# A linear-attention and MLP kernel: other dummy matmuls at the start, input loads in larger pieces, one bias load moved behind the transposes

## The chip, the cores and the metric

The kernel runs on one core of one Trainium2 chip. The metric is the device time of one execution in microseconds (us). The profile gives, for one profiled execution, the span from the first to the last instruction of the core, and the start and length of every instruction and DMA packet.

Engines are named as in the profile: PE (TensorE matmuls), PEld (its weight loads), DVE (VectorE), ACT (ScalarE), POOL (GpSimd), SP (SyncE, which here only issues DMAs). "SPq" and "ACTq" are the instruction queues of SP and ACT when they issue a DMA.

## The reference

One sequence of 2048 rows and 512 columns in bf16 passes through four residual steps, A, B, A, B, with the same weights in both rounds:

```python
x = x + A(layernorm(x))     # linear attention, 32 heads of 16
x = x + B(layernorm(x))     # layernorm again, 512 -> 1792, gelu, 1792 -> 512
x = x + A(layernorm(x))
x = x + B(layernorm(x))

# A: q, k, v = y @ wqkv; phi(t) = (t > 0 ? t + 1 : exp(t)) + 1e-6
#    kv = phi(k)^T v, z = sum of phi(k) over the rows
#    o = phi(q) kv / (phi(q) z + 1e-6); A = o @ wo
# B: gelu(layernorm(y) @ w1 + b1) @ w2 + b2
```

The sums over all rows in kv and z mean that phi(k) of every row has to be there before any row of A's output can be made.

## The kernel before

The 2048 rows are 16 tiles of 128 rows, four tiles to a chunk of 512. Everything stays in on-chip memory between the steps. The work is recorded as a graph of operations, and the order of the operations on each of the five engines is written out as five lists of names in `CONF["ORDER"]` (from line 325). The program plays each list in that order and inserts a semaphore wait wherever an operation reads or overwrites what another engine or a DMA made. A scheduling pass with estimated durations only gives out buffers and PSUM banks; it changes no order. So an operation that waits holds up everything behind it in its engine's list, SP's list of DMAs included.

Only the first stage, the attention half of the first round, matters for what follows. Names end in the tile number (12 to 15 first, since chunk 3 is taken first, then 0 to 11):

- **The loads.** SP issues, in this order: `x0` (tile 12, 128 KB, line 642), `x1` (tile 13, 128 KB, line 644), `wk0` (half of the key columns of wqkv, 256 KB, line 648), `x2` (tiles 14 and 15, 256 KB), `wq` (all query columns, 512 KB, line 651), and the three other chunks of x, `xc0` to `xc2` (512 KB each, line 638). ACT issues the second half of the key columns, `wk1`, after DVE has written `onesm`.
- **The dummies.** `warm` (lines 678 to 682) is the first entry of PE's list: seven matmuls of 128x512 and one of 128x128 on the tile `onesm`, whose result nobody reads. `onesm` is filled with 1.0 by DVE (`ones`, line 641), so `warm` waits for DVE.
- **Norm and turn.** For each tile the statistics are made on DVE (or ACT), the tile is centred or normalised, and it is then transposed ("turned"): tiles 12, 13, 14, 15 and 1 by PE (`PTA0_n`, line 783, copied out by ACT in `tcA0_n`, line 793), the eleven others by a DMA transpose that SP issues (`TA0_n`, line 770).
- **Keys and queries.** `K0_n` (line 838, four matmuls of 128x512) makes the keys of a tile. `Q0_c_k` (lines 856 and 869) makes queries. ACT makes exp and relu of the result (lines 808 and 819), DVE or POOL joins them to phi (`mink`, `phik`, lines 812 to 825).
- **Sums.** `G0_n` (line 939) multiplies the normalised tile with phi(k) and accumulates in four PSUM banks; `Z0_c` (line 920) sums phi(k). `zb0` (line 1000) prepares the denominators, for which `D0_...` (line 1063) are the first matmuls.
- **SP's list in this stage**, after the loads: `TA0_0 TA0_3 TA0_2 TA0_8 TA0_4 b2 TA0_6 TA0_7 TA0_5 TA0_10 TA0_11 TA0_9 b1 Tb1`. Here `b2` (line 1193) loads the bias b2 into all partitions (128 KB); it is first read by `b20_1`, which starts at 64.5 us.
- **Late loads.** wv, wo, w1 and w2 are issued by POOL (line 665) once all turns of the stage have landed.

After this stage PE's list holds the output of the attention (line 1087), the two MLP matmuls (lines 1119 and 1157) and the second round, in one mixed order.

Of the kernel before, what the change touches and what calls it, by code (L numbers as in the profile page):

```python
# [264 lines left out]
def assign_waits(graph, order, sems, dma_sems):  # L265
# [56 lines left out]
    C0=(3, 0, 1, 2), N_WARM=7, ZC=(0, 3), LQ='sp', N_HALF=1, N_K=4, N_Q=3, P_Z0=6.15, N_PB=1, N_PT=8, P_DEN=-50.43,  # L322
    P_A2=-55.11, P_W1=38.59, P_W2=10.23, P_K=55.79, P_G=131.85, P_Q=170.13, STEP=3.86, A1_Q=12.91, A1_STEP=0.5, N_H=4,
    N_N=3, GAP=28.61,
    ORDER={
        "pe":
            "warm PTA0_12 PTA0_13 K0_12 K0_13 PTA0_14 Q0_3_0 Q0_3_2 PTA0_15 K0_14 G0_12_0 Q0_3_1 K0_15 G0_13_0 "
            "G0_14_0 Q0_3_3 PTA0_1 K0_0 K0_1 G0_15_0 K0_3 G0_0_0 K0_2 Q0_0_2 Q0_0_0 G0_1_0 K0_8 Z0_3 K0_4 G0_2_0 "
            "K0_6 G0_3_0 Q0_0_3 K0_7 K0_5 G0_4_0 K0_10 K0_11 Z0_0 K0_9 Q0_1_2 Q0_1_3 Z0_1 Q0_0_1 Q0_1_0 Z0_2 "
            "G0_5_0 G0_6_0 D0_0_3 D0_0_0 G0_7_0 Q0_1_1 D0_0_1 G0_8_0 D0_0_2 G0_9_0 G0_10_0 G0_11_0 G0_11_2 G0_11_1 "  # L330
            "D0_1_0 Q0_2_0 G0_11_3 KV0_0 KV0_1 D0_1_1 ZR0 KV0_2 KV0_3 Q0_2_1 D0_1_2 M0_0 M0_1 M0_2 M0_3 Q0_2_2 "
            "WO0_0_0 WO0_0_1 WO0_0_2 WO0_0_3 D0_1_3 WO0_1_0 WO0_2_0 WO0_3_0 Q0_2_3 WO0_4_0 WO0_7_0 WO0_6_0 PTB0_0 "
            "WO0_5_0 W10_0_5_0 W10_0_1_0 W10_0_9_0 W10_0_6_0 W10_0_2_0 W10_0_3_0 W10_0_12_0 W10_0_7_0 W10_0_0_0 "
            "W10_0_4_0 W10_0_13_0 W10_0_11_0 W10_0_8_0 W10_0_10_0 W20_0_0 W20_1_0 W20_0_7 W20_1_7 W10_0_9_1 "
            "W10_0_1_1 W10_0_7_1 W10_0_8_1 W10_0_5_1 W10_0_6_1 W10_0_12_1 W10_0_0_1 W10_0_13_1 W10_0_3_1 "
            "W10_0_11_1 W10_1_4_0 W10_1_13_0 W10_0_4_1 W10_1_11_0 W10_1_0_0 W10_1_3_0 W10_1_2_0 W10_0_2_1 "
            "W10_1_6_0 WO0_9_0 WO0_8_0 WO0_11_0 W10_1_5_0 W10_1_8_0 W10_1_10_0 WO0_10_0 W10_0_10_1 W10_1_1_0 "
            "W10_1_12_0 W10_1_7_0 W10_1_9_0 W20_7_0 W20_4_0 W20_7_7 W20_4_7 WO0_15_0 W20_5_0 W20_2_0 W20_5_7 "
            "W20_6_0 W10_2_5_0 W10_2_0_0 K1_1 W20_6_7 W20_2_7 K1_0 W10_2_11_0 W10_2_10_0 WO0_12_0 WO0_14_0 "
            "WO0_13_0 W10_2_3_0 W10_2_13_0 W10_2_4_0 W10_2_2_0 W10_2_1_0 W10_2_6_0 W10_2_12_0 W10_2_9_0 W10_2_8_0 "  # L340
            "W10_2_7_0 W20_8_0 W20_9_0 W20_8_7 W20_9_7 W20_3_0 W20_10_0 K1_4 W20_3_7 K1_2 W20_10_7 W10_3_5_0 "
            "W20_11_0 W10_3_7_0 W10_3_1_0 W10_3_8_0 W10_3_3_0 W10_3_10_0 W10_3_0_0 W20_11_7 W10_3_9_0 K1_3 "
            "W10_3_6_0 W10_3_13_0 W10_3_2_0 K1_8 W10_3_11_0 W10_3_12_0 W10_3_4_0 K1_5 G1_0_1 G1_0_3 K1_6 G1_0_0 "
# [6 lines left out]
            "W11_0_1_0 W11_0_7_0 W11_0_9_0 WO1_7_0 W11_0_8_1 W11_0_4_1 W11_0_10_1 W11_0_8_0 W11_0_1_1 W11_0_5_1 "  # L350
# [23 lines left out]
            "gelu0_1_1_0 gelu0_1_9_0 gelu0_0_10_1 gelu0_1_7_0 gelu0_1_12_0 normB0_11 normA1_1 normB0_9 expk1_1 "  # L374
            "expk1_0 gelu0_2_10_0 reluk1_0 gelu0_2_5_0 gelu0_2_0_0 gelu0_2_3_0 gelu0_2_11_0 gelu0_2_13_0 "
            "gelu0_2_2_0 gelu0_2_4_0 gelu0_2_1_0 gelu0_2_6_0 gelu0_2_8_0 gelu0_2_12_0 normB0_13 gelu0_2_7_0 "
            "gelu0_2_9_0 normA1_2 expk1_2 reluk1_2 reluk1_4 gelu0_3_7_0 gelu0_3_1_0 gelu0_3_8_0 normA1_5 normA1_6 "
            "gelu0_3_0_0 gelu0_3_3_0 gelu0_3_5_0 gelu0_3_9_0 gelu0_3_10_0 reluk1_3 normA1_7 gelu0_3_6_0 "
            "gelu0_3_2_0 expk1_3 expk1_8 expk1_4 gelu0_3_13_0 gelu0_3_11_0 gelu0_3_4_0 gelu0_3_12_0 expk1_5 "
            "reluk1_8 expk1_6 reluk1_6 normA1_9 normA1_10 expk1_7 reluk1_7 normA1_11 expk1_9 expk1_10 reluk1_10 "  # L380
# [4 lines left out]
            "expq1_2_1 expq1_2_0 expq1_3_3 reluq1_2_0 reluq1_2_1 normB1_1 tcB1_1 reluq1_3_3 tcB1_0 gelu1_0_13_0 "  # L385
# [12 lines left out]
            "statsA0_15 mink0_12 yscA0_13 aggrA0_15 phik0_12 cenA0_15 mink0_13 vepsA0_14 statsA0_0 minq0_3_0 "  # L398
# [3 lines left out]
            "statsA0_7 normA0_4 aggrA0_7 phiq0_3_1 aggrA0_10 mink0_3 statsA0_5 mink0_2 aggrA0_5 phik0_2 phik0_3 "  # L402
            "statsA0_9 aggrA0_9 zs0_3 statsA0_11 aggrA0_11 mink0_8 minq0_3_3 mink0_4 phik0_8 phiq0_3_3 phik0_4 "
            "normA0_9 minq0_0_2 normA0_11 phiq0_0_2 mink0_6 mink0_7 phik0_7 minq0_0_3 phiq0_0_3 mink0_5 zs0_0 "
            "phik0_5 mink0_10 phik0_10 minq0_0_0 mink0_11 phik0_11 zs0_1 mink0_9 minq0_1_2 phik0_9 phiq0_0_0 "
# [3 lines left out]
            "RA0_4 normB0_0 minq0_2_2 minq0_2_1 RA0_7 b20_1 phiq0_2_1 RA0_5 statsB0_7 minq0_2_3 statsB0_5 "  # L409
# [21 lines left out]
            "normB1_0 rec1_1_3 statsB1_3 pr1_1_3 minq1_3_3 RA1_5 aggrB1_3 normB1_2 RA1_4 normB1_3 RA1_6 pz1_3_1 "  # L431
            "phiq1_3_2 red1_3_1 statsB1_5 statsB1_4 RA1_7 aggrB1_4 statsB1_6 den1_3_1 rec1_3_1 aggrB1_5 statsB1_7 "
            "minq1_2_0 minq1_2_1 aggrB1_7 phiq1_3_3 aggrB1_6 phiq1_2_0 red1_3_0 den1_3_0 red1_3_2 pr1_3_1 den1_3_2 "
            "pz1_2_0 normB1_5 rec1_3_0 red1_2_0 phiq1_2_1 red1_3_3 rec1_3_2 pz1_2_1 minq1_2_3 RB1_3 den1_3_3 "
            "pr1_3_0 RB1_0 den1_2_0 minq1_2_2 pr1_3_2 phiq1_2_3 pz1_2_3 rec1_2_0 red1_2_1 pr1_2_0 b21_1 phiq1_2_2 "
            "red1_2_3 RA1_13 den1_2_3 b21_5 den1_2_1 rec1_3_3 pr1_3_3 rec1_2_3 rec1_2_1 RB1_1 pz1_2_2 red1_2_2 "
            "RA1_14 den1_2_2 statsB1_13 rec1_2_2 pr1_2_2 RA1_12 statsB1_12 aggrB1_12 RB1_2 RA1_11 statsB1_14 "
            "RA1_15 statsB1_15 aggrB1_14 RA1_10 normB1_14 RA1_8 aggrB1_15 statsB1_10 statsB1_11 aggrB1_13 RA1_9 "
            "aggrB1_10 statsB1_8 normB1_13 statsB1_9 aggrB1_11 aggrB1_9 b21_7 b21_13 RB1_7 aggrB1_8 b21_12 RB1_4 "
            "normB1_8 normB1_10 RB1_5 b21_6 b21_8 b21_9 RB1_6 RB1_12 RB1_14 RB1_10 RB1_9 RB1_8 b21_11 RB1_13 "  # L440
            "RB1_11 RB1_15_0 RB1_15_1",
        "pool":
            "bdm0 id0 id1 neghalf powA0_12 vepsA0_13 powA0_13 powA0_14 eps6 vepsA0_0 powA0_15 b1z powA0_0 vepsA0_1 "
            "vepsA0_3 powA0_3 nmrA0_3 powA0_1 vepsA0_6 vepsA0_2 powA0_2 vepsA0_8 powA0_6 powA0_8 nmrA0_8 nmrA0_6 "
            "vepsA0_4 powA0_4 vepsA0_7 vepsA0_10 powA0_7 nmrA0_7 powA0_10 vepsA0_5 powA0_5 nmrA0_10 nmrA0_5 "
            "vepsA0_11 vepsA0_9 powA0_11 powA0_9 phik0_6 wo w2_1 bdm1 wv w1_1 w2_0 w1_0 phiq0_1_2 phiq0_1_1 "
            "pr0_0_2 pr0_1_0 pr0_1_1 pr0_1_2 pr0_1_3 vepsB0_1 powB0_1 vepsB0_0 powB0_0 pz0_2_1 vepsB0_2 phiq0_2_3 "
            "powB0_2 vepsB0_7 vepsB0_3 powB0_7 powB0_3 vepsB0_5 vepsB0_6 powB0_5 powB0_6 vepsB0_4 powB0_4 pr0_2_1 "
            "phiq0_2_2 b20_0 b20_3 b20_2 b20_5 vepsB0_9 vepsB0_8 vepsA1_0 powB0_8 powB0_9 vepsA1_1 powA1_0 pr0_3_3 "
            "vepsB0_10 powA1_1 pz0_3_2 vepsB0_11 nmrB0_9 powB0_11 nmrB0_11 powB0_10 nmrA1_1 b20_9 pr0_3_1 vepsA1_7 "  # L450
            "vepsA1_4 vepsB0_14 vepsB0_15 vepsB0_13 powB0_14 powB0_13 vepsB0_12 vepsA1_2 vepsA1_5 powA1_7 nmrB0_13 "
            "powB0_15 powA1_4 powB0_12 powA1_2 b20_8 b20_12 nmrA1_2 powA1_5 vepsA1_9 powA1_9 nmrA1_5 vepsA1_8 "
            "vepsA1_6 powA1_8 powA1_6 nmrA1_7 nmrA1_9 nmrA1_6 vepsA1_3 powA1_3 za1_1 vepsA1_10 za1_3 vepsA1_11 "
            "powA1_10 nmrA1_10 phik1_6 powA1_11 za1_5 phik1_7 nmrA1_11 vepsA1_13 powA1_13 za1_7 vepsA1_12 za1_8 "
            "powA1_12 nmrA1_12 za1_9 za1_10 vepsA1_14 vepsA1_15 powA1_14 powA1_15 za1_11 phik1_15 pz1_1_0 pr1_0_0 "
# [72 lines left out]
def build_kernel(nc, A_x, A_wqkv, A_wo, B_x, B_w1, B_b1, B_w2, B_b2, out, conf=None, report=False):  # L528
# [5 lines left out]
    with ExitStack() as es:  # L534
# [143 lines left out]
        def warm(e):  # L678
            for n in [D] * cf["N_WARM"] + [P]:
                ins = e.matmul(bank(wu, n), lhsT=onesm[:, 0:P], rhs=onesm[:, 0:n], start=True, stop=True)  # L680
# [671 lines left out]
```

## Time and profile before

| what | us |
|---|---|
| median of three runs | 329.73 |
| lowest and highest of them | 328.83, 329.91 |
| the profiled execution: its own time | 330.35 |
| its span | 328.6 |
| first matmul of `warm` starts | 1.51 |
| first turn on PE (`PTA0_12`) starts | 4.59 |
| `wk0` lands, `K0_12` starts | 6.43, 6.52 |
| `x0`, `x1`, `x2`, `wq` land | 3.21, 3.93, 6.95, 8.45 |
| last turn of the stage lands (`TA0_9`) | 36.95 |
| last matmul starts its stream, last DVE operation ends | about 325.8, 326.5 |

Around the span the profiled execution has 1.75 us more, which is start and end of the program.

How to read the views. The chain of work is followed back from the last instruction: at each step to what released it. A row of it is start, length, engine and line. A row of the timeline is start, length, engine, line, operation, the tiles written and read, shape and count, and in brackets the idle time of the engine before it with what ended that. The table by stretches gives for each engine the busy time and in brackets the number of instructions that started. A matmul's length in the timeline includes a modelled drain, so rows of PE overlap; how fast PE really goes is read from the distance between the starts.

### The profile page before, as it was taken

To read this page: it belongs to the slowest core of one execution; us is meant where nothing else is said; L and a number is where in the kernel's file an instruction comes from. 1 tells how busy PE (TensorE), PEld (TensorE's weight loads), DVE (VectorE), ACT (ScalarE), POOL (GpSimd) and SP (SyncE) were. 2 spreads that over 40 slices of the span, in tenths; PEclk is the share of its full clock that TensorE was granted. 3 is DMA by queue.
4 is the path that set the end of the run, shared out by engine and by line. 5 is a ranking of instruction groups with operands and counts; after the bars stand their busy time and mean duration, and the time that the engine had idled before them with its cause. 6 is when DMAs were issued, how large, how long until landed. Compare 5 with 4: busy or idle time off the path is not lost.

```text
span 328.6 us, 4769 instructions
## 1 busy us (share of the span) xinstructions
PE 322.0 (98%) x1716; PEld 159.1 (48%) x1716; DVE 223.0 (68%) x507; ACT 194.4 (59%) x334; POOL 133.1 (41%) x223
## 2 busy tenths in 40 slices
PE   7999999999999999999999999999999999999996
PEld 2444545476544444444444444448644444444444
DVE  4799599999794554575158899999989776100132
ACT  4898769783747055536984377878933452567200
POOL 3366646567447105533047725756903176000000
PEclk9999999999999999999999999999999999999999
DMA  6324593105404300312101110022044214200011
GB/s 231 152 49 98 121 358 149 18 16 97 49 0 66 80 16 3 64 32 48 34 16 32 35 32 0 2 49 50 18 96 99 48 33 97 64 0 2 16 48 64
DMA packets 47027, 20.37 MB, mean 62 GB/s; under 512 B 41948, under 2 KB 45532, under 8 KB 47004
## 3 DMA queue, kind: packets, MB, share of 16 engines
q1 hardware_dynamic: 45676, 15.09, 20.7%
q0 software_dynamic: 1056, 4.72, 4.1%
q8 instruction: 13, 0.21, 0.3%
q10 hardware_dynamic: 272, 0.26, 0.3%
q14 instruction: 10, 0.08, 0.1%
HBM read 8.00 MB, written 2.10 MB: 31 GB/s over the span
## 4 chain that ended last, share of the span: by engine, by line
PE 94%; DMA 2%; DVE 1%; ACT 1%; issue 0%; SPq 0%; ACTq 0%
PE ps L1119 30%; PE ps L1157 29%; PE ps L838 9%; PE ps L1087 8%; PE ps L856 5%; PE ps L971 4%; PE ps L939 3%; PE ps L869 2%; DMA wqkv<-in_A_wqkv_dram 1%; DMA t<-yb 1%; PE ps L1144 1%; PE ps L1063 1%; PE ps L1017 1%; PE ps L994 1%; PE ps L783 0%
## 5 line engine op out<-in xcount | busy, mean ns | idle before, releaser
L1125 ACT ACTIVATE gT<-ps,b1c 128x512 bf16<-128x512 f32 (+1 forms) x140 | 77.0, 601 | 53.8 <-PE ps L1119 53.3
L1119 PE MATMUL ps<-t,w 128*128 128x512 bf16 (+1 forms) x560 | 101.3, 336 | 0.4 <-issue 0.4
L1157 PE MATMUL ps<-w,gT 128*128 128x512 bf16 x434 | 97.3, 379 | 0.0
L1119 PEld LDWEIGHTS ps<-t,w 128*128 128x128 bf16 x560 | 54.6, 98 | 43.6 <-ACT t L793 1.2
L1157 PEld LDWEIGHTS ps<-w,gT 128*128 128x128 bf16 x434 | 42.5, 98 | 50.8
L808 ACT ACTIVATE eb<-ps 128x512 bf16<-128x512 f32 x56 | 32.5, 602 | 31.0 <-PE ps L838 25.6
L735 POOL TENSOR_TENSOR rstd<-veps,neghalf 128x1 f32<-128x1 f32 x64 | 37.8, 598 | 8.3 <-DVE veps L733 5.9
L1167 DVE TENSOR_TENSOR outb<-ps,xsb 128x512 bf16<-128x512 f32 x15 | 10.2, 683 | 40.2 <-PE ps L1157 38.7
L838 PE MATMUL ps<-wqkv,t 128*128 128x512 bf16 x128 | 33.6, 394 | 1.4 <-DMA t<-yb 0.7
L720 DVE BATCH_NORM_STATS2 stats<-xsb 128x6 f32<-128x512 f32 x48 | 32.0, 680 | 0.3
L1087 PE MATMUL ps<-gtb,t 128*128 128x512 bf16 x128 | 30.9, 379 | 0.0
L760 DVE TENSOR_SCALAR yb<-xsb,mv,rstd 128x512 bf16<-128x512 f32 x28 | 16.7, 602 | 13.6 <-POOL rstd L735 13.4
L733 POOL TENSOR_SCALAR veps<-mv 128x1 f32<-128x1 f32 x28 | 7.4, 276 | 43.7 <-DVE mv L722 43.0
L755 ACT ACTIVATE yb<-xsb,nmr,rstd 128x512 bf16<-128x512 f32 x20 | 15.7, 811 | 14.6 <-POOL nmr L752 14.6
L819 ACT ACTIVATE rb<-ps 128x512 bf16<-128x512 f32 x38 | 21.8, 601 | 0.2 <-PE ps L838 0.2
L821 DVE TENSOR_SCALAR eb<-eb 128x512 bf16<-128x512 bf16 x46 | 14.4, 325 | 10.1 <-ACT eb L808 10.0
L725 POOL TENSOR_SCALAR veps<-mv 128x1 f32<-128x1 f32 x32 | 8.8, 274 | 29.1 <-DVE mv L722 27.2
L838 PEld LDWEIGHTS ps<-wqkv,t 128*128 128x128 bf16 x128 | 12.3, 100 | 17.0 <-issue 1.7
L856 PE MATMUL ps<-wqkv,t 128*128 128x512 bf16 x80 | 20.3, 383 | 0.0
L1163 DVE TENSOR_TENSOR xsb<-ps,xsb 128x512 f32<-128x512 f32 x16 | 11.0, 688 | 13.2 <-PE ps L1157 13.1
L1087 PEld LDWEIGHTS ps<-gtb,t 128*128 128x128 bf16 x128 | 12.3, 98 | 15.1 <-DVE mv L722 0.5
L1104 POOL TENSOR_TENSOR xsb<-xsb,b2b 128x512 f32<-128x512 f32 x14 | 17.4, 1255 | 2.8 <-ACT yb L755 1.6
(103 smaller groups left out, 395.2 us busy)
## 6 DMA issues: line engine op xcount, KB each, us to landing
w<-in_B_w_dram POOLq DMA_DIRECT2D x4, 896.0 KB, 9.8
out_dram<-outb SPq DMA_DIRECT2D x15, 128.0 KB, 2.0
t<-in_A_x_dram SPq DMA_DIRECT2D x3, 512.0 KB, 7.3
t<-yb SPq DMA_TRANSPOSE x56, 2.5
wqkv<-in_A_wqkv_dram SPq DMA_DIRECT2D x1, 512.0 KB, 5.8
wo<-in_A_wo_dram POOLq DMA_DIRECT2D x1, 512.0 KB, 4.6
wqkv<-in_A_wqkv_dram POOLq DMA_DIRECT2D x1, 512.0 KB, 7.4
t<-t SPq DMA_TRANSPOSE x20, 2.5
```

Of the source, the lines that this page charges most:

```text
L720: G.op("dve", lambda e: e.bn_stats(stats[:, s.slot, :], src()), 620, reads=src_keys, writes=[k + "s"], tiles=[s, *src_tiles], prio=prio, n ...
L735: G.op("pool", lambda e: e.tensor_tensor(rstd[:, s.slot:s.slot + 1], veps[:, s.slot:s.slot + 1], neghalf[:], op=ALU.pow), 570, reads=[k + ...
L760: G.op("dve", lambda e: e.tensor_scalar(yb[:, y.slot, :], src(), stats[:, s.slot, 2:3] if by_act else mv[:, s.slot, 0:1], rstd[:, s.slot:s ...
L808: G.op("act", lambda e: e.activation(eb[:, et.slot, :], bank(bt), ACT.Exp, scale=factor()), 478, reads=[src_key, *more], writes=[f"e{tag}" ...
L819: G.op("act", lambda e: e.activation(rb[:, rt.slot, :], bank(bt), ACT.Relu, scale=factor()), 478, reads=[src_key, *more], writes=[f"r{tag} ...
L838: ins = e.matmul(bank(b), lhsT=yTa(yT)[:, dt, k * P:(k + 1) * P], rhs=wqkv[:, dt, D:2 * D], start=(dt == 0), stop=(dt == DT - 1))
L856: ins = e.matmul(bank(b), lhsT=yTa(yT)[:, dt, k * P:(k + 1) * P], rhs=wqkv[:, dt, 0:D], start=(dt == 0), stop=(dt == DT - 1))
L1087: ins = e.matmul(bank(wb), lhsT=yTa(pq)[:, kt, k * P:(k + 1) * P], rhs=gtb[:, kt, :], start=(kt == 0), stop=(kt == DT - 1))
L1104: G.op("pool" if on_pool else "dve", lambda e: e.tensor_tensor(xsb[:, st, :], xsb[:, st, :], b2b[:], op=ALU.add), 1120 if on_pool else 600 ...
L1119: ins = e.matmul(bank(b, n), lhsT=w1[:, dt, ft * P:(ft + 1) * P], rhs=yTa(yT)[:, dt, k0 * P:k1 * P], start=(dt == 0), stop=(dt == DT - 1))
L1125: G.op("act", lambda e, ft=ft, b=b, k0=k0, k1=k1, n=n: e.activation(gT[:, g.slot, ft * 512 + k0 * P:ft * 512 + k1 * P], bank(b, n), ACT.Ge ...
L1157: ins = e.matmul(bank(b), lhsT=gT[:, g.slot, ft * 512 + k * P:ft * 512 + (k + 1) * P], rhs=w2[:, ft, :], start=(ft == 0), stop=(ft == FT - 1))
```

## The change

Four things change in the first stage.

1. The dummy matmuls read a constant 1.0 that the program's preamble holds in memory (one element, read over and over) in place of `onesm`, so `warm` waits for nobody. There are eight of 128x512 and two of 128x128. Two more dummy groups stand in PE's list: `idle0_0`, one of 128x128, behind the first turn `PTA0_12`, and `idle0_1`, two of 128x128, behind the second turn `PTA0_13`. PE's list begins `warm PTA0_12 idle0_0 PTA0_13 idle0_1 K0_12 K0_13 PTA0_14`.
2. x comes by pairs: `x0` is tiles 12 and 13 in one DMA of 256 KB, `x2` is tiles 14 and 15 as before; `x1` is gone. A row in memory is then 2 KB in place of 1 KB for the first pair.
3. `wk0` and `wk1` each carry the query columns too: 512 KB each in rows of 2 KB, in place of 256 KB in rows of 1 KB; `wq` is gone. SP's list begins `x0 wk0 x2 xc0 xc1 xc2`.
4. `b2` no longer stands between `TA0_4` and `TA0_6` in SP's list: it waits for all turns and follows `Tb1`.

Besides, the five lists differ by swaps of close neighbours in many places (for instance `Q0_3_3` before `G0_14_0`, `W20_11_0` four places later, `OD12` before `OD14`); no list gains or loses any other operation. Line numbers after the first third of the file are 1 to 7 higher.

```diff
-        self.parts = {..., "wk": ("wk_0", "wk_1")}
+        self.parts = {..., "wk": ("wk_0", "wk_1"), "wq": ("wk_0", "wk_1")}
...
-    C0=(3, 0, 1, 2), N_WARM=7, ...
+    N_WARM2=2, N_IDLE=(1, 2), C0=(3, 0, 1, 2), N_WARM=8, ...
...
-        dma("sp", lambda e: e.dma_start(x0ap(HC, 0), rows(x_dram, HC)[:, 0, :]), [("x0", FIRST)], ...name="x0", kb=128)
-        for k, n in ((1, 1), (2, 2)):
-            dma("sp", ...rows(x_dram, HC)[:, k:k + n, :]...name=f"x{k}", kb=128 * n)
+        def load_pair(k, prio):
+            dma("sp", ...rows(x_dram, HC)[:, k:k + 2, :]...name=f"x{k}", kb=256, rate=440.0)
+        load_pair(0, -120)
         for h, q in enumerate(("sp", "act")):
-            dma(q, lambda e, h=h: e.dma_start(wqkv[:, 2 * h:2 * h + 2, D:2 * D], wsrc[:, 2 * h:2 * h + 2, D:2 * D]), ...
+            dma(q, lambda e, h=h: e.dma_start(wqkv[:, 2 * h:2 * h + 2, 0:2 * D], wsrc[:, 2 * h:2 * h + 2, 0:2 * D]), ...
+        load_pair(2, -98)
         load_chunk(cf["LQ"], C0[1], -98)
-        dma(cf["LQ"], lambda e: e.dma_start(wqkv[:, :, 0:D], wsrc[:, :, 0:D]), ["wq"], prio=-97, name="wq", kb=512)
...
-        def warm(e):
-            for n in [D] * cf["N_WARM"] + [P]:
-                ins = e.matmul(bank(wu, n), lhsT=onesm[:, 0:P], rhs=onesm[:, 0:n], start=True, stop=True)
+        def run_idle(e, sizes):
+            one = nc.const_aps.tensor(1.0, [P, D], BF16)
+            for n in sizes:
+                ins = e.matmul(bank(wu, n), lhsT=one[:, 0:P], rhs=one[:, 0:n], start=True, stop=True)
             return ins
...
+        idle("warm", [D] * cf["N_WARM"] + [P] * cf["N_WARM2"])
...
-                    tr = transpose_pe(y, ykey, yT, k, f"yT0_{st}", pr, f"A0_{st}", True)
+                    wait = [held] if held else ()
+                    tr = transpose_pe(y, ykey, yT, k, f"yT0_{st}", pr, f"A0_{st}", True, wait)
+                    held = idle(f"idle{n}_{k}", [P] * cf["N_IDLE"][k], ...) if n == 0 and k < 2 else None
...
-                    dma("sp", lambda e: e.dma_start(b2b[:], ...), ["b2b"], prio=-79, name="b2", kb=128, after=[tr])
...
+        dma("sp", lambda e: e.dma_start(b2b[:], ...), ["b2b"], prio=-79, name="b2", kb=128, after=trs)
```

## The prediction, made before the changed kernel was run

> **What bounds the kernel now.** I read the page's shares first, then the chain of work in order of time, then those stretches of the timeline in which the chain leaves PE. The shares:
>
> ```profile
> PE 322.0 (98%) x1716; PEld 159.1 (48%) x1716; DVE 223.0 (68%) x507; ACT 194.4 (59%) x334; POOL 133.1 (41%) x223
> PE 94%; DMA 2%; DVE 1%; ACT 1%; issue 0%; SPq 0%; ACTq 0%
> ```
>
> PE is busy for 98% of the span and carries 94% of the chain. So a change in one stage is worth what it takes from PE's idle time, or from the time in which PE goes slowly; later stages only move along. The chain shows both in the first stage:
>
> ```profile
> 1.72 4.71 DMA wqkv<-in_A_wqkv_dram
> 6.43 0.09 issue
> 6.52 3.57 PE ps L838 x8
> ...
> 15.30 0.86 PE ps L838 x4
> ...
> 27.20 3.32 DMA t<-yb
> 30.52 0.14 issue
> 30.66 1.02 PE ps L838 x4
> ...
> 44.85 0.69 DVE zb L1000
> 45.54 0.05 issue
> ```
>
> The first real matmuls (`K0_12`, `K0_13`) wait for the key weights until 6.43 us. Then eight matmuls take 3.57 us, 0.43 each by their starts; from 15.30 on four take 0.86, that is 0.216 each. PE starts at half pace. By stretches of 3.41 us (columns: busy time and in brackets instructions of PE, PEld, DVE, ACT, POOL, granted clock, DMA share, GB/s):
>
> ```profile
> 0.65:4.06 3.41, 2.55 (x7) 0.90 (x8) 1.28 (x3) 1.39 (x2) 1.35 (x4) 1.00 0.39 117
> 4.06:7.47 3.41, 2.71 (x14) 1.27 (x13) 1.83 (x7) 2.51 (x6) 0.80 (x2) 1.00 1.04 347
> 7.47:10.89 3.42, 3.42 (x13) 1.49 (x12) 2.50 (x9) 1.60 (x3) 0.75 (x2) 1.00 1.03 418
> 10.89:14.30 3.41, 3.41 (x21) 1.61 (x20) 2.39 (x10) 3.41 (x7) 1.10 (x4) 1.00 0.10 40
> ```
>
> The clock column says 1.00 in all four and is no help here; the counts are: 13 matmuls in the third, 21 in the fourth, PE busy throughout both. The pace doubles near 10.9 us. The dummies with the first turn were an unbroken run of 3.49 us (1.51 to 5.00) and did not raise it; the run from 6.52 did, after 4.4 us.
>
> The third place is PE's wait before `K0_6`, for a turn that SP issued late:
>
> ```profile
> 28.92 1.03 PE L939 MATMUL ps<-pkb,yb 128*128 128x512 bf16 x4
> 30.66 0.59 PE L838 MATMUL ps<-wqkv,t 128*128 128x512 bf16 x2 [0.71 <-DMA t<-yb]
> ```
>
> ```profile
> 25.34 1.19 SPq L770 DMA_TRANSPOSE t<-yb  x1
> 26.57 0.58 SPq L1193 DMA_DIRECT2D b2b<-in_B_b_dram  x1
> 27.20 4.43 SPq L770 DMA_TRANSPOSE t<-yb  x3
> ```
>
> PE's stream would have gone on at 28.92 + 0.86 = 29.78, so the hole is 30.66 - 29.78 = 0.88 us. SP issues `b2` in the middle of the turns, back to back with them.
>
> **The change part by part.**
>
> *b2 behind the turns.* `TA0_6` is issued at 26.57 in place of 27.20; its data (ACT, 24.95 to 25.76) are there. It took 3.32 us to land while b2's 128 KB moved; the median of the 56 turns is 2.5. So it lands between 26.57 + 2.5 = 29.07 and 26.57 + 3.32 = 29.89; PE starts 0.14 later, at 29.21 to 30.03, against 29.78. The gain is between 0.63 and 0.88; I take 0.88, since with b2 away the median row is the nearer one. What is late next: `TA0_5` waits for its own data until 30.41 and lands at 32.90 as before, `K0_5` then wants it at 34.11 - 0.88 = 33.23; `TA0_9` lands at 36.95 and `K0_9` wants it at 37.97 - 0.88 = 37.09. That holds, with 0.14 to spare, so no more than 0.88 can come out here unless all turns move. b2 itself is covered: it is read at 64.5 us and would be issued near 38.6; without that cover it would cost what its landing exceeds that, nothing in sight. Further on PE waits 0.6 us at 45.5 for `zb0`, behind two DVE operations that took 1.37 and 1.24 us, where their likes take 0.41 and 0.28, while POOL worked. If PE and DVE come earlier and POOL's DMA issues do not, that collision falls elsewhere: between the stall's whole loss (-0.6) and one more slowed operation (+0.96). I take 0.
>
> *Larger first loads.* Before `K0_12` can start, x0, x1 and both key halves had to land, 768 KB; now it is the first pair and both joint loads, 1280 KB. Nearest row below: all of x0, x1, wk and x2, 1024 KB, had landed at 6.95. The other 256 KB take 0.75 us at 347 GB/s or 0.63 at 418 (the stretches' rates with 1 KB and 4 KB rows). Against that, SP issues the weights 0.47 earlier (1.25, not 1.72), and the 1024 KB themselves, at a rate between the two, save up to 0.5. So 6.6 to 7.7, and I take 6.85: `K0_12` at 6.95, 0.4 later. The far bound is by proportion to bytes: 1.25 + 4.71 x 1280 / 768 = 9.1. The path pays between half of the delay (the pace doubles at the same instant, so what is displaced runs later at double pace) and all of it (the doubling moves along): 0.2 to 0.4, I take 0.2. That wq comes sooner is worth 0: it landed at 8.45 and its first reader started at 10.31, behind other matmuls. The pair makes tile 12 wait for tile 13: x0 landed at 3.21, x1 at 3.93, the pair then between, some 0.4 later for the first turn (5.0, not 4.59); `tcA0_12` ends at 6.25 in place of 5.85, still before the weights.
>
> *Dummies.* PE can start near 0.85 (SP and ACT start at 0.79 and 0.80). Eight of 0.427 and two of 0.107 last 3.63 us, to 4.48, before the first turn could start: cost 0. The three small ones behind the turns take 0.11 and 0.21 us in holes of 0.3 (before the second turn) and 0.6 us (before `K0_12`): cost 0, or 0.2 if the weights landed by 6.3. What they bring depends on when the pace doubles. The unbroken run is 3.63 us. The rows have 3.49, which failed, and 4.4, which did it; 3.63 is nearer to the one that failed. So I take no change of pace, and keep the other case as a rival.
>
> [...]
>
> *Swaps.* From 66 us on PE's holes in this trace come to some 0.4 us in all, so the swaps can gain 0.4; a misplaced one could cost one waiting matmul group, 0.2 to 0.9. I take 0.
>
> **Sum.** Profiled execution 330.35 - 0.88 + 0.2 = 329.7. The median of the runs lies 0.62 below the profiled execution, so 329.05; call it 329.0.
>
> **Rivals.**
>
> *A, the pace doubles before `K0_12`.* For: PE's start would be busy from 0.85 on with holes of half a us, where before it had 1.5 us of nothing and a hole of 0.8. Against: the row of 3.49 us. Then `K0_12`, `K0_13`, the third turn and `Q0_3_0` run at 0.216 in place of 0.427, but not all of it reaches the end: ACT is busy without a break from 10.56, when it copies out the third turn, and that turn needs x2, landing at 6.95 before and some 0.3 later now, plus 1.36 us of statistics and centring: 8.7 in place of 9.89. So 1.1 us, not the 2 that PE saves, against the 0.2 lost: 330.35 - 0.88 - 1.1 = 328.4, by the median 327.7.
>
> *B, the forecast:* 328.6 to 329.8.
>
> *C, slower: the joint weights land late and the pace waits with them.* Place: `K0_12`'s wait for wk. If the doubling needs its 4.4 us counted from `K0_12`, every us of delay is paid in full. It beats b2's gain from a delay of 0.88, that is a start at 7.4; at the far bound of 9.2 it is 2.7 - 0.88 = +1.8, 331.5 by the median. For: two thirds more bytes stand before the first matmul, and the slowest of the DMA engines, not the mean rate, ends the wait. Against: rows of 2 KB and an earlier issue.
>
> **Numbers.** Chances: B 0.46, A 0.34, C 0.20. A measurement of this kernel tells about 0.3%, 1.0 us, from no change. All of A but a little, and the lower edge of B, are more than 1.0 below 329.73: faster 0.41. The rest of B and C's mild part: same 0.42. C's far part, or a misplaced swap: slower 0.17. Range: A's 327.7 less 0.4 for the spread of the runs, 327.3; above B far into C, 330.5.
>
> **What would show it.** b2: no wait of PE for a turn near 29 us, `TA0_6` landing about 2.5 us after its issue. Loads: the start of the first line-843 matmul, 6.95, with 7.4 as C's mark. Dummies: distance of the starts among those eight matmuls, 0.427 for B and 0.216 for A, and the time at which it changes. A stall moved: PE waiting for `TA0_9` or for `zb0` by more than 0.6 us. I am wrong if the weights land past 7.4, or if the pace doubles before the weights.

## The result, and the profile after

The changed kernel takes 334.37 us (median of six runs, 331.23 to 335.52); the kernel before, run in turn with it, 329.13 (328.18 to 329.91). The ratio is 1.015, with a 95% interval of 1.0103 to 1.0197: slower. The profiled execution took 335.52 us, span 333.8, against 330.35 and 328.6 before: 5.17 us more. The forecast was 329.0 with a range up to 330.5, so it was wrong in sign and size.

PE's share, first as busy time, then of the chain. PE is busy for less of the span, and DVE and DMA have taken over part of the chain:

```profile
PE 320.8 (96%) x1689; PEld 159.2 (48%) x1721; DVE 225.4 (68%) x507; ACT 194.6 (58%) x334; POOL 132.4 (40%) x223
PE 84%; DVE 8%; DMA 4%; issue 2%; ACT 1%; SPq 0%; ACTq 0%
```

(The count of 1689 is short of some matmul records; the changed kernel has five matmuls more, not 27 fewer.)

The chain of work of the changed kernel, cut to the first stage (start, length, what):

```profile
1.49 7.85 DMA wqkv<-in_A_wqkv_dram
9.33 0.09 issue
9.42 3.57 PE ps L843 x8
...
16.04 0.86 PE ps L843 x4
...
29.90 3.91 DMA t<-yb
33.81 0.14 issue
33.94 1.02 PE ps L843 x4
```

Two things are to be seen. The second half of the joint weights, issued by ACT at 1.49, needs 7.85 us where half its bytes needed 4.7 us before, so `K0_12` starts at 9.42, 2.90 later. And the turn `TA0_6` takes 3.91 us to land, although `b2` no longer moves beside it. The table by stretches, now with the edges at which the granted clock changes, 4.41, 7.82 and 14.65, and steps of 3.41 us (PE, PEld, DVE, ACT, POOL, clock, DMA share, GB/s):

```profile
1.00:4.41 3.41, 3.41 (x10) 1.22 (x8) 1.18 (x3) 1.80 (x3) 1.16 (x3) 1.00 0.65 214
4.41:7.82 3.41, 1.13 (x13) 0.62 (x11) 1.31 (x6) 1.78 (x4) 1.08 (x3) 1.00 0.99 365
7.82:11.24 3.41, 1.81 (x5) 0.74 (x6) 1.83 (x4) 0.00 (x0) 0.32 (x1) 0.50 0.82 335
11.24:14.65 3.41, 3.41 (x13) 1.49 (x11) 1.22 (x5) 2.46 (x5) 0.00 (x0) 0.50 0.02 7
```

The dummies did raise the pace, at 4.41: the turns in the second row go at 0.056 us a matmul. In that row PE worked for only 1.13 of 3.41 us, since it waited for the weights, and from 7.82 the clock is 0.50 for two stretches. All eight matmuls of `K0_12` and `K0_13` run at 0.427 again. PE's rows around `K0_6`, and SP's row there:

```profile
32.24 1.03 PE L944 MATMUL ps<-pkb,yb 128*128 128x512 bf16 x4
33.94 1.02 PE L843 MATMUL ps<-wqkv,t 128*128 128x512 bf16 x4 [0.67 <-DMA t<-yb]
```

```profile
27.24 7.71 SPq L775 DMA_TRANSPOSE t<-yb  x5
```

SP issues nothing but turns now, yet the hole is 33.94 - (32.24 + 0.86) = 0.84 us, as good as the 0.88 before. Up to here the changed kernel is 3.3 us behind. The rest comes at a place that the prediction did not look at, before the MLP group `W10_1_4_0`; first PE's rows in the changed kernel, then in the kernel before at the same work:

```profile
83.77 2.24 PE L1124 MATMUL ps<-t,w 128*128 128x256 bf16 x19
87.87 1.24 PE L1124 MATMUL ps<-t,w 128*128 128x512 bf16 x5 [1.86 <-ACT gT L1130]
```

```profile
80.82 3.42 PE L1119 MATMUL ps<-t,w 128*128 128x256 bf16 x23
```

PE stands still for 2.03 us (85.84 to 87.87), where before it went through. The view names ACT's `gT`, but that had been done for half a us. `W10_1_4_0` also reads the turn `TB0_6`, issued at 82.42 and landed at 87.56: 5.14 us, where the median of all turns is 2.48. What the DMA engines did while it was in flight, from 84.4 to 86.9 us in 40 slices of 0.0625 us, and the instruction queues in that time:

```profile
GB/s 21 8 262 0 0 0 0 0 0 61 143 221 213 225 233 201 217 184 135 168 37 8 4 4 20 12 8 8 12 12 74 0 0 0 4 9 9 8 4 0
q14 instruction: 1, 0.01, 2.5%
q8 instruction: 1, 0.02, 2.3%
```

The lone 262 is one packet of 16 KB on the instruction queue q8, at 84.54; it takes 0.94 us. The turns' packets stop, come back for 0.7 us, and trickle at 0 to 20 GB/s from 85.7 on, but for one slice of 74, when an 8 KB instruction packet (q14) moves. There are 13 such 16 KB packets in each of the two executions, 79 to 138 recorded matmuls apart. The trace does not tell what they carry. With 2 x 1716 PE instructions (a matmul and a weight load each) 13 x 16 KB is 62 bytes for each, one packet for 132 matmuls, so I read them as fetches of PE's program, an estimate from these counts; "fetch" below means such a packet. The three kernels below with 13 to 29 matmuls more than the kernel before (c4, c5, d4) have 14 of them. In the kernel before one came at 81.26, 2.37 us after the issue of `TB0_6` (78.89), which had just about landed (81.45) untouched; the two turns behind it took 4.63 and 3.76 us, but nobody waited for them. In the changed kernel it comes 2.12 us after the issue.

Over all turns of tiles in the two executions (`Tb1`, 4.61 and 4.50 us with no 16 KB packet, is left aside): of 124 turns that no 16 KB packet overlaps, none took over 2.95 us; of the 28 that one overlaps, 16 took 2.99 to 5.14 us. `TA0_6` is among these in both kernels (packets at 27.64 and 30.85).

### The profile page after: what moved, and what is told of

Read it like the earlier page. It is cut to its first block, busy times and chain, and to the rows that moved or that the text cites. A ratio compares the mean times of both kernels' runs of the same rounds, so it can differ in the third digit from the quotient of the medians.

```text
span 333.8 us, 4742 instructions
## 1 busy us (share of the span) xinstructions
PE 320.8 (96%) x1689; PEld 159.2 (48%) x1721; DVE 225.4 (68%) x507; ACT 194.6 (58%) x334; POOL 132.4 (40%) x223
## 4 chain that ended last, share of the span: by engine, by line
PE 84%; DVE 8%; DMA 4%; issue 2%; ACT 1%; SPq 0%; ACTq 0%
PE ps L1124 27%; PE ps L1162 26%; PE ps L843 8%; PE ps L1092 6%; PE ps L861 4%; PE ps L976 4%; PE ps L944 3%; DMA wqkv<-in_A_wqkv_dram 2%; PE ps L874 2%; DMA t<-yb 1%; PE ps L1149 1%; DVE eb L826 1%; PE ps L1068 1%; DVE t L1056 1%; DMA t<-t 1%
## 5 line engine op out<-in xcount | busy, mean ns | idle before, releaser
L813 ACT ACTIVATE eb<-ps 128x512 bf16<-128x512 f32 x56 | 32.5, 601 | 32.2 <-PE ps L843 25.6
L1092 PE MATMUL ps<-gtb,t 128*128 128x512 bf16 x124 | 30.1, 379 | 0.4 <-DMA t<-t 0.3
L826 DVE TENSOR_SCALAR eb<-eb 128x512 bf16<-128x512 bf16 x46 | 15.5, 343 | 12.2 <-ACT eb L813 11.9
```

The source lines that it names most:

```text
L813: G.op("act", lambda e: e.activation(eb[:, et.slot, :], bank(bt), ACT.Exp, scale=factor()), 478, reads=[src_key, *more], writes=[f"e{tag}" ...
L826: G.op("dve", lambda e: e.tensor_scalar(eb[:, et.slot, :], eb[:, et.slot, :], 1.0, 1e-6, op0=ALU.min, op1=ALU.add), 210, reads=[f"e{tag}"] ...
L1092: ins = e.matmul(bank(wb), lhsT=yTa(pq)[:, kt, k * P:(k + 1) * P], rhs=gtb[:, kt, :], start=(kt == 0), stop=(kt == DT - 1))
```

## The experiments

Three theories. LOADS: the joint load on ACT's queue lands late, and `K0_12` waits. DUMMIES: the early dummies raise the pace, and PE's idle time loses it again. FETCH: an instruction fetch that falls on a turn in flight holds it up, and any change in the number or the time of PE's instructions moves that collision.

### Parts alone

The kernel before on the same chip took 328.66 us (35 runs, 327.83 to 332.28).

**e1_after_split**: the changed kernel, key and query weights separate again.

```diff
-e.dma_start(wqkv[:, 2*h:2*h+2, 0:2*D], ...)      # both halves, 512 KB
+e.dma_start(wqkv[:, 2*h:2*h+2, D:2*D], ...)      # 256 KB, and wq behind x2
```

> The changed kernel with its joint key and query loads undone: wk0 and wk1 carry the key columns alone again (256 KB each), wq is its own load of 512 KB behind x2. Dummies, pairs of x, the late b2 and all swaps stay. Theory LOADS (the second joint half, issued by ACT, lands at 9.33 us because it shares the DMA engines with all that SP has queued, and K0_12 waits for it): K0_12 starts at 6.5 to 6.8 again, 2.9 us earlier, the pace doubles up to 3.4 us earlier, and the time falls by about 3.3, to 331. Rival DUMMIES (the cost is that the pace rises at 4.4 us and is taken back at 7.8): the time stays above 333. Theory FETCH (a 16 KB instruction fetch near 84.5 us holds up the turn TB0_6, for which PE waits 2 us) says nothing of the loads; the 2 us may stay or go with a shift of a quarter of a us.

330.16 us, ratio 1.0027 (0.9997 to 1.0057). The weights landed at 6.57, `K0_12` started near 6.66 at 0.216, and the full clock of 4.54 held. So some 4 us of the loss go with the joint loads and the pace. But the wait before `W10_1_4_0` stayed, with `TB0_6` at 5.01 us and a fetch 2.05 us behind its issue:

```profile
82.72 1.46 PE L1125 MATMUL ps<-t,w 128*128 128x512 bf16 x6 [1.74 <-ACT gT L1131]
```

**e2_before_joint**: the kernel before, joint loads alone.

```diff
-e.dma_start(wqkv[:, 2*h:2*h+2, D:2*D], ...)      # and wq
+e.dma_start(wqkv[:, 2*h:2*h+2, 0:2*D], ...)      # both halves, 512 KB
```

> The kernel before with the joint loads alone. LOADS: K0_12 starts near 9.4, and the time rises by about 3.3, to 332.4. DUMMIES: no change, 329.1.

330.87 us, ratio 1.0062 (1.0031 to 1.0092): slower by 2.2 in the median, not 3.3. Both halves land late here, ACT's at 8.54 and SP's, the last, at 8.75, ahead of x2 (9.30). The chain shows SP's half and half pace behind it:

```profile
1.71 7.04 DMA wqkv<-in_A_wqkv_dram
8.75 0.09 issue
8.84 3.57 PE ps L837 x8
```

**e3_before_b2**: the kernel before, `b2` behind the turns.

```diff
-TA0_4 b2 TA0_6 ... b1 Tb1 TB0_1
+TA0_4 TA0_6 ... b1 Tb1 b2 TB0_1
```

> The kernel before with b2 behind the turns alone. The prediction's account (b2's transfer makes TA0_6 late): TA0_6 lands about 2.5 us after its issue, the hole of 0.88 us before K0_6 goes, 328.3. FETCH: the instruction fetch at 27.6 us still meets TA0_6 in flight, which again takes over 3 us; the hole stays for the most part, within 0.3 of the time before.

329.12 us, ratio 0.9998 (0.9966 to 1.003): nothing. `TA0_6` took 4.12 us without `b2` (fetch at 26.09, issue at 24.66), and the wait before `K0_6` remained (the view names DVE, but the turn landed at 28.78):

```profile
28.92 1.02 PE L838 MATMUL ps<-wqkv,t 128*128 128x512 bf16 x4 [0.88 <-DVE pkb L814]
```

This profile has the wait before `W10_1_4_0` too. PE stands still for 2.13 us, and `TB0_6` took 5.01 us, with a fetch 1.94 us behind its issue (76.97):

```profile
82.29 1.89 PE L1119 MATMUL ps<-t,w 128*128 128x512 bf16 x9 [1.97 <-ACT gT L1125]
```

PE's list is here that of the kernel before, without one matmul more. What differs ahead of the wait is the place of `b2` and the pace, which rose at 4.90 in place of 10.89. So the wait is not the changed kernel's alone: the timing of an execution can bring it.

**e4_before_dummies**: the kernel before, the new dummies alone (`warm`, `idle0_0` and `idle0_1` as in the change).

```diff
-"warm PTA0_12 PTA0_13 K0_12 ..."                 # seven wide and one small, on onesm
+"warm PTA0_12 idle0_0 PTA0_13 idle0_1 K0_12 ..." # eight wide and two small, on the constant
```

> The kernel before with the new dummies alone. DUMMIES: 2 us slower or more. LOADS: not slower; with the weights at 6.4 the pace may rise at some 4.4 us and hold, which would make it up to 1.1 faster, or be taken back in some runs: 328 to 329.4. FETCH: five more matmuls move every later instruction fetch some 0.5 us earlier against the work, which may put one on a turn that PE needs: +2 if so.

329.37 us, ratio 1.001 (0.9982 to 1.0038); that median counts one run of 1934.68 us, and is 329.27 without it. In the profile the start is as rival A had it, but 1.5 us are given back at `W10_1_4_0`, where `TB0_6` took 4.39 us:

```profile
5.99 1.89 PE L843 MATMUL ps<-wqkv,t 128*128 128x512 bf16 x8
...
81.32 1.89 PE L1124 MATMUL ps<-t,w 128*128 128x512 bf16 x9 [1.37 <-ACT gT L1130]
```

This profile also shows `b2` by itself. `TA0_6`, issued right behind `b2` at 25.04, took 3.21 us with no instruction packet in flight, and PE stood still for 0.76 us before `K0_6` (the view's figure is less, because of the modelled drain):

```profile
28.39 1.02 PE L843 MATMUL ps<-wqkv,t 128*128 128x512 bf16 x4 [0.59 <-DMA t<-yb]
```

### Without DMA transposes: the start by itself

These kernels replace each DMA transpose by a plain DMA of the same tile. Their data are not transposed, and b1 is replaced by a piece of wo, so they leave out that part of the computation; everything else stays. SP issues such a copy in 0.65 us in place of 1.3 (`b2`, a plain DMA of 128 KB, took 0.58 in the kernel before; four transposes took 5.20 in the changed kernel), so turns land earlier against PE.

**c1_copy_before**, the base:

```diff
-return e.dma_start_transpose(dst, yb[:, y.slot, :])
+return e.dma_start(dst, yb[:, y.slot, :].rearrange("p (d s) -> p d s", d=DT))
```

> The kernel before with every DMA transpose replaced by a plain DMA of the same tile from the same source to the same place (512 pieces of 256 bytes), and b1's turn by a small load from wo: what is left out is the transposition of the turns that SP issues, and b1. Waits, lists and all other work stay. It is the base for the next three. FETCH (a 16 KB instruction fetch holds up a turn in flight): if that is a thing of DMA transposes alone, no copy takes over 3 us, the waits of 0.88 us before K0_6 and any wait at W10_1_4_0 are gone and the time falls by 1 to 2 us, to about 327.5; if a fetch holds up any DMA, copies that meet one land 1 to 2 us later than the others. LOADS and DUMMIES: the first 10 us as in the kernel before: K0_12 near 6.5, half pace until 8 to 14 us.

327.27 us (326.80 to 328.55). The copy for `K0_6` met a fetch (issue 24.97, fetch 26.14) and took 3.9 us, and PE waited 0.92 us for it. The answer on the DMA issues from 24.9 to 25.6 us:

```profile
t<-yb SPq DMA_DIRECT2D x1, 128.0 KB, 3.9
```

So plain DMAs that a fetch overlaps land late as well. Over c1 to c4: of 264 copies that no 16 KB packet overlaps the slowest took 2.48 us (median 2.30); of the 40 that one overlaps, 20 took 3.03 to 4.48.

**c2_copy_after**: the changed kernel with the same copies (diff as c1).

> The changed kernel with the same plain copies in place of the DMA transposes (the transposition of these turns and b1 are left out). LOADS: wk1 lands past 9 us and K0_12 starts near 9.4 as in the changed kernel, so against the kernel before with copies it loses about 3 us (2.9 at the start, less or more by the clock), and nothing of the 1.8 at W10_1_4_0. FETCH with copies untouched by fetches: the difference of the two kernels with copies is 3.0 to 3.5, not the 5.2 of the profiled pair. [...]

330.84 us (328.10 to 331.81): 3.57 above c1, not 5.2, and no wait at `W10_1_4_0`. In its profile the same ten dummies, started at the same 0.83, did **not** raise the pace, which rose at 12.99. Counted back from there in steps of 3.41 us, the stretches begin at 2.75 and 6.16, and PE was busy for 2.57 and 1.55 us of them:

```profile
2.75:6.16 3.41, 2.57 (x13) 1.31 (x12) 1.68 (x6) 0.78 (x3) 0.55 (x1) 1.00 0.94 332
6.16:9.57 3.41, 1.55 (x10) 0.76 (x8) 2.18 (x5) 1.77 (x4) 0.94 (x3) 1.00 1.03 409
```

`K0_12` started at 8.67 at half pace, which lasted to 12.99. Two of its twelve runs took 328.1 and 328.25; in seven others the mean granted clock is 0.990 or 0.995, which I read as half clock for two or one stretches of 3.41 us (in the changed kernel's profile 6.83 us at 0.50 make 0.990).

**c3_copy_after_sp**: c2, both halves issued by SP ahead of x2.

```diff
-for h, q in enumerate(("sp", "act")):            # SP: x0 wk0 x2 ...
+for h, q in enumerate(("sp", "sp")):             # SP: x0 wk0 wk1 x2 ...
```

> The changed kernel with copies, and one edit more: both joint weight loads are issued by SP, in the order x0, wk0, wk1, x2; ACT issues none. LOADS as queue sharing (the half that ACT issued got what SP's queue left over): wk1 lands at 7 to 7.6 us in place of 9.33, K0_12 starts near 7.7, and the time lies 1.7 or more below the changed kernel with copies. If it is the bytes alone (1280 KB ahead of the first matmul at this rate): wk1 lands at 8.7 or later and the time is the same. DUMMIES: PE's idle time from 5.8 us shrinks from 3.6 to below 2; where the full clock of 4.4 us then survives, K0_12 runs at 0.216 and the time falls by about 1 more.

328.24 us (327.27 to 329.72), 2.6 below c2. The same bytes landed at 6.76 in place of 8.58, and the idle stretch shrank. Its trace has no record of the clock, so the pace is read from the starts: the last wide dummy starts at 3.77, the next matmul 0.27 us later, so the pace doubles near 3.88, and `K0_12` still has it. An estimate of the stretch behind that edge, with PE busy for 1.84 (its clock column says nothing here):

```profile
3.88:7.29 3.41, 1.84 (x18) 0.99 (x17) 2.03 (x7) 2.02 (x5) 0.66 (x1) 1.00 1.04 385
```

```profile
6.85 1.89 PE L843 MATMUL ps<-wqkv,t 128*128 128x512 bf16 x8 [0.33 <-ACT t L798]
```

So it is not the bytes alone. In c2 the half on ACT's queue landed behind the x2 that SP had issued after it (7.57); in one queue it landed ahead of x2 (7.39). The queue and the place ahead of x2 change together here; which of the two counts was not told apart. The mean granted clock is 0.995 in three of the twelve runs.

**c4_copy_after_fill**: c2, eight wide dummies more behind the second turn.

```diff
-idle(..., [P] * cf["N_IDLE"][k], ...)
+idle(..., [P] * cf["N_IDLE"][k] + ([D] * 8 if k else []), ...)
```

> The changed kernel with copies, and one edit more: idle0_1 behind the second turn has eight dummies of 128x512 more, which fill 1.7 us (full clock) to 3.4 us (half) of PE's wait for the weights from 5.8 to 9.42 us. The loads are untouched: K0_12 starts near 9.4. DUMMIES (the full clock of 4.4 us was taken back at 7.8 because PE stood idle): the clock stays at 1.0 past 7.8 us, the eight matmuls of K0_12 and K0_13 run at 0.216 in place of 0.427, and the time lies 1 to 2 us below the changed kernel with copies. If the clock falls whatever PE does, they stay at 0.427 and the time is the same. LOADS: wk1 still lands past 9 us.

328.99 us (327.96 to 330.31), 1.85 below c2, though the weights landed at 9.30 in its profile. With PE busy in both stretches the clock stayed, in this profile and, by the mean clock (0.999 or more), in all twelve runs:

```profile
5.08:8.49 3.41, 2.71 (x19) 1.33 (x19) 1.42 (x7) 1.78 (x4) 1.06 (x3) 1.00 1.00 350
8.49:11.90 3.41, 2.52 (x15) 1.33 (x16) 1.91 (x5) 1.46 (x3) 0.34 (x1) 1.00 0.73 296
```

```profile
9.39 1.89 PE L843 MATMUL ps<-wqkv,t 128*128 128x512 bf16 x8 [0.97 <-issue]
```

Four more, on another chip.

**c1b_copy_before_again**: c1 unchanged.

> The kernel before with plain copies in place of the DMA transposes, once more, unchanged, as the base on the same chip for the next three (the transposition of these turns and b1 are left out). All theories: about 327.3 us as in its first measurement. FETCH: copies that no 16 KB instruction fetch meets take 2.3 us, those that meet one up to 4 us; the copy ahead of K0_6 is met again (fetch near 26 us) and PE waits 0.9 us there.

327.26 us (326.88 to 328.93): the base repeats to 0.01 in the median. The copy for `K0_6` was met again (3.83 us, wait 0.83).

**c5_copy_before_narrow**: c1, the dummies cut into narrow ones, 21 PE matmuls more in the same time.

```diff
-for n in [D] * cf["N_WARM"] + [P]:
+for n in [P] * (4 * cf["N_WARM"] + 1):
```

> The kernel before with plain copies, and one edit: the dummies of warm are 29 matmuls of 128x128 in place of seven of 128x512 and one of 128x128. The columns that PE goes through, the start and the end of warm stay; there are 21 PE matmuls more. FETCH: the first fetch comes about 21 matmuls earlier against the work, near 21 to 23 us in place of 26.14, and no longer meets the copy for K0_6 issued at 24.97: that one lands in 2.3 us, the wait of 0.92 us before K0_6 goes, and the time falls by about 0.9 to 326.4. If the fetch falls on the copies issued at 22.24 or 23.66 instead, the wait is before K0_8 or K0_4, at 0.9 to 1.2, and the time stays. DUMMIES and LOADS: the same time and the same wait before K0_6.

328.59 us (327.41 to 330.08): 1.3 slower, not 0.9 faster. The fetch came at 17.58, earlier than expected, and the wait before `K0_6` did go. But it met the copy issued at 16.45 (3.71 us), for 0.44 us of wait there, and later fetches met others: 0.71 us at 224 us. The first half of FETCH held: the first thirteen of its fourteen fetches all came earlier than those of c1, by 1.4 to 8.6 us. The second half, that it can be moved to where it costs nothing, did not. The copy for `K0_6`, beside `b2` and met by no fetch, took 3.00 us.

**c6_copy_before_dummies**: c1, the new dummies alone (diff as e4).

> The kernel before with plain copies, and the new dummies alone (eight of 128x512 and two of 128x128 on the constant, from 0.83 us, three small ones behind the first two turns). DUMMIES: the full clock comes near 4.4 us in most runs and K0_12 runs at 0.216; the start gains where the base had half pace until 8 to 14 us and nothing where the base had the full clock by 6: 326.5 to 327 in the median, with less spread than the base. FETCH: the base of copies does not lose 1.5 us at W10_1_4_0, since its copies are issued early enough; so here, unlike in the kernel with transposes, the gain of the start reaches the end. LOADS: K0_12 at 6.0 to 6.5.

326.96 us (326.27 to 327.29, seven runs): at most 0.3 below the base, within the spread of the runs.

**c7_copy_after_split**: c2, separate weights (diff as e1).

> The changed kernel with plain copies, and one edit: the key and the query weights are loaded separately again (256 KB halves of the key columns, then wq), as in the kernel before. Dummies, pairs of x, late b2 and the order stay as changed. LOADS: K0_12 starts at 6.4 to 6.7 in place of 8.7 to 9.4, the clock is not taken back, and the time lies 3.0 to 4.0 us below the changed kernel with copies (330.84): 326.8 to 327.8, level with the base. If the joint loads are not the cause, it stays above 329.5. FETCH: nothing lost at W10_1_4_0.

326.93 us (326.08 to 329.26): 3.9 below c2 (on another chip, where the base took the same time) and 0.3 below the base. So the whole loss of c2 hangs on the joint loads, and by c4 about half of it on the pace that is lost while PE waits for them. Dummies, pairs of x, late `b2` and the swaps together are worth 0.3 or nothing.

### Halves: SP's pace of before, and the wait at W10_1_4_0

Whole copies are issued too fast for that wait. Here each turn is two plain DMAs of half a tile, 1.3 us a turn (what is left out is the same as in c1).

```diff
-return e.dma_start(dst, ...)
+U: e.dma_start(dst[:, :, 0:64], ...)
+T: e.dma_start(dst[:, :, 64:128], ...)           # next in SP's list
```

**d1_half_before**

> The kernel before with each DMA transpose replaced by two plain DMAs of half the tile each (512 pieces of 128 bytes), issued one behind the other, and b1's turn by a small load from wo: what is left out is the transposition of the turns that SP issues, and b1. SP takes some 1.3 us for a turn again, as with the transposes. All theories: 328 to 330 us. FETCH: halves met by a 16 KB instruction fetch land up to 2 us later than the others; the fetch near 79 to 81 us falls just behind the turn TB0_6 or on it: a wait of 0 to 1 us before W10_1_4_0. LOADS and DUMMIES: K0_12 near 6.5.

335.43 us (335.01 to 336.92). No wait at `W10_1_4_0`: the fetch came at 81.77, when the first half of `TB0_6` had landed (81.14) and the second nearly (82.01), and PE's row runs through:

```profile
79.28 8.09 PE L1124 MATMUL ps<-t,w 128*128 128x256 bf16 x55
```

The level is 8 us higher than with whole copies, other turns being late all over, more than I expected.

**d2_half_after**

> The changed kernel with the same halves in place of the transposes (their transposition and b1 are left out). FETCH: the wait of 1.5 to 2 us before W10_1_4_0 is back if the fetch near 82 to 84 us falls on TB0_6's halves in flight, and the kernel loses 5 us against the kernel before with halves; if it misses them, the wait is away and the loss is 3.3 to 3.6, as with whole copies. A turn that is merely issued too late would show a normal landing of 2.3 to 2.6 us and a wait all the same. LOADS and DUMMIES: K0_12 near 9, and the 3.3 to 3.6 of the start in any case.

340.27 us (338.94 to 341.61), 4.84 above d1, where c2 stood 3.57 above c1. The wait is back, with the fetch at 83.70 on the second half of `TB0_6`. Its chain:

```profile
82.64 3.66 DMA t<-yb
86.31 0.27 issue
86.58 1.46 PE ps L1129 x6
```

PE waited 1.32 us; 4.84 - 3.57 = 1.27. That these agree so closely is partly luck, since the runs of a kernel spread over 2 to 4 us and one of them is profiled.

**d3_half_after_split**

> The changed kernel with halves and with the key and query weights loaded separately again. LOADS: 3 to 4 us below the changed kernel with halves. FETCH: the number of PE instructions ahead is that of the changed kernel, so the same turn is met as there: the wait before W10_1_4_0 has the same length within 0.5 us, though the start is 3 us earlier. If the wait came from turns issued too late against PE, it would be longer here than in the changed kernel.

337.18 us (336.44 to 338.87), 3.1 below d2. `K0_12` starts at 6.92 (8.33 in d2) and the full pace comes for good at 10.72 (14.35), and the same turn is met all the same (80.02, fetch at 81.10, 3.27 us), with a wait of 0.93 us:

```profile
83.56 3.62 PE L1130 MATMUL ps<-t,w 128*128 128x512 bf16 x18 [0.77 <-DMA t<-yb]
```

Here the clock was taken back for one stretch although the loads are separate; PE had been busy for 1.79 us of the stretch before:

```profile
3.89:7.31 3.41, 1.79 (x17) 0.96 (x16) 2.31 (x8) 1.77 (x5) 0.66 (x1) 1.00 0.98 328
7.31:10.72 3.41, 3.41 (x12) 1.46 (x11) 2.44 (x9) 2.10 (x6) 0.76 (x2) 0.50 1.01 414
```

**d4_half_after_split_narrow**: d3 with `N_WARM=0, N_WARM2=34`, 24 matmuls more in the same time.

> As the one before it (halves, separate weights), and one edit more: warm is 34 matmuls of 128x128 in place of eight of 128x512 and two of 128x128, the same PE time with 24 matmuls more. FETCH: the fetch near 78 us comes about 24 matmuls (2.6 us) earlier and falls on another turn; the wait before W10_1_4_0, if the one before it has one, goes or is under 0.5 us, and another may come up where a turn with little to spare is met. If the wait came from turns issued too late, it stays as it is, within 0.2 us.

337.85 us (336.59 to 339.99). The fetch came at 78.47. `TB0_6` landed normally (2.2 and 2.5 us for its halves) and nobody waited for it. But the fetch met the turn `TB0_3`, and PE waited 0.78 us for that one:

```profile
76.46 4.01 DMA t<-yb
80.47 0.05 issue
80.52 3.56 PE ps L1130 x31
```

So the wait follows the fetch, not the turn. (The start differs too: `K0_12` at 7.76, and half clock from 6.92 to 13.75.) A kernel with the DMA transposes themselves in which only PE's instruction count differs was not tried.

## Why the prediction was wrong, point by point

- **Larger first loads** (taken: landing 6.85, `K0_12` at 6.95, cost 0.2) is the step that failed most. It added the missing 256 KB at the mean rate, as if the engines served the weights first. They landed at 9.33, even past its far bound of 9.1 by bytes, since ACT's half ended among what SP had issued behind its own (x2 landed at 8.13, `xc0` at 9.82). With the same bytes in one queue they land at 6.76 (c3), close to the 6.85. The far bound's 7.85 us, by proportion to bytes, is just what ACT's half took in the profiled execution. That is luck: with the same list of loads it landed at 8.58 (c2), 9.30 (c4) and 8.24 (d2). The term measures +3.9 (c2 against c7), the pace included.
- **Dummies, "no change of pace"**: wrong as a step, since it compared lengths of runs (3.49 failed, 4.4 did it). In the profiled execution 3.58 us from 0.83 did it, at 4.41; in c2 the same run did not. PE's busy time in the 3.41 us up to an edge orders the profiles better: with wide dummies the pace rose after stretches with PE busy for 2.95 us (c4) to 3.41 (the changed kernel), not after 2.79 (c1b) or less, and the stretches begin elsewhere in each execution (1.00 and 4.41 in the changed kernel, 2.75 and 6.16 in c2). The pace was lost again after stretches in which PE was busy for 1.13 (the changed kernel), 1.29 (d2), 1.63 (d4) and 1.79 us (d3) of 3.41, while 1.84 (c3, by the estimate) and 1.99 (c6) kept it. That it can be lost again stood in no term of the sum, and it is what happened in at least five of the changed kernel's six runs (mean clock 0.990 or less, 1.0 in the run of 331.23).
- **What an early pace brings**: rival A's 1.1 us is not reached (its 328.4 also leaves out the 0.2 that it names as lost). Where the pace holds and nothing else is changed, 0.3 (c6) or nothing (e4) is left. A reason shows in the profiles: the old dummies (narrow in c5), too, raise the pace by 6.5 us in four of seven (e3, c1, c5, d1), and only in three at 10 to 14 (before, e2, c1b); the new ones do it in ten of eleven, and lose it again in four of these. I had taken the one execution of before for the rule. In the kernel with transposes the rest is given back at `W10_1_4_0`.
- **b2** (taken: -0.88): wrong as a gain. The hole stayed at 0.84, and the change alone gave 0.9998. The 3.32 us of `TA0_6` had been put down to `b2` alone; the instruction fetch at 27.64 moved beside it too. Either is enough: with `b2` and no fetch the turn takes 3.21 us (e4; as a plain copy 3.00 in c5, 2.96 in c6), with a fetch and no `b2` 3.58 to 4.12 (e1, the changed kernel, e3), with neither 2.35 as a copy (c4). So taking one of the two away gave nothing.
- **Not in the sum at all**: 1.3 (d2) to 2.0 us (the profiled pair) for the turn `TB0_6`. "Later stages only move along" was the false premise. They move along with PE, but the fetches moved with PE's instruction count (with 24 matmuls more, from 81.10 in d3 to 78.47 in d4) and the turns with SP. How much of the 5.2 us between the medians this is stays open: e3 has the wait with PE's list of before, so some executions of the kernel before may have it too, and one of each was profiled.
- **Rival C** had place and mechanism right (a start past 7.4, the pace waiting with the weights), and the price per us of delay. It missed the rest because it still credited `b2` with 0.88 and knew nothing of the fetch: 2.7 - 0.88 = 1.8 became about 3.3 + 1.9 = 5.2.
- **Swaps and pairs of x** (taken: 0): with the dummies and late `b2` they come to -0.3 in c7; alone they were not tried.

Left open: why a turn that meets a fetch takes up to 2.7 us longer when the packet itself takes 0.9 to 1.7. In the changed kernel an 8 KB instruction packet followed at 85.60. Over the six profiles with transposes, turns met by a 16 KB packet alone (61) have a median of 2.56 and reach 4.53 us, those met by both (25) have a median of 4.05 and reach 5.14; no run was made that separates the two. That the collisions also make the spread of a kernel's runs is likely, not shown.

## What to carry to other kernels

Before the first matmul count what the other queues have in flight, not only the bytes ahead: here ACT's half of the weights landed at 9.33 us, behind the x2 that SP had issued after it (8.13), and only one queue, in order, put the weights first (6.76 in c3). The early dummies kept their pace where PE was busy until the real work came (c4, 1.85 us below c2); it was given back where PE was busy for 1.13 to 1.79 of the next 3.41 us. And before a slow DMA is put down to its neighbour, look at the instruction queues in the trace: here the collision with a fetch fell on another transfer when the instruction count changed (`TB0_3` in place of `TB0_6` in d4) and met `TB0_6` in flight with PE's list unchanged (5.01 us in e3, 2.56 in the kernel before). Both causes may hold, and then removing one shows nothing (`b2`, ratio 0.9998).

## What the runs showed of the hardware

- DMAs in flight that a 16 KB packet on an instruction queue overlapped, transposes and plain copies alike, took 3 to 5.1 us in half of the cases (16 of 28 turns in the pair, 20 of 40 copies in c1 to c4); the median of all turns is 2.48, that of the copies that none overlapped 2.30. Elsewhere three turns took 3.2 us without one: two met an 8 KB packet of the other instruction queue (e2, e3), one moved beside `b2` (e4). Of the half turns of d1 to d4 that met no 16 KB packet, three took over 3 us (3.33 to 3.36), each beside an 8 KB packet.
- The fourth of these packets came after 445 to 467 recorded matmuls in every profile, the first after 77 to 132, less fixed than I expected; the thirteenth came after 1558 to 1562, whatever the kernel (1590 in the kernel before, whose trace has 31 matmul records more than the others with its list).
- The recorded changes of the granted clock lie a whole number of 3.41 us apart within an execution: 4.41, 7.82 and 14.65 in the changed kernel, 10.89 and 328.33 (93 steps) in the kernel before, 7.31 and 10.72 in d3, 6.92 and 13.75 in d4. Their phase differs between executions: 4.41 in the changed kernel and 12.99 in c2 with the same PE list are 2.51 steps apart.
- PE's busy time in a stretch does not order all profiles: with narrow dummies the clock rose after 2.68 (d4) and 2.78 us (c5), with wide ones not after 2.79 (c1b).
